# Sparse attention and a PReLU layer pair: a shorter result ring, local q and k turned by transfers, layer-1 order

## The chip, the cores and the metric

The kernel runs on one core of a Trainium2 chip. A core has TensorE (PE, matrix products into the accumulation memory PSUM), VectorE (DVE), ScalarE (ACT), GpSimd (POOL) and SyncE (SP), each with its own instruction queue, and transfers (DMA) that SP and POOL issue. The metric is the device time of one execution in microseconds (us); less is better.

## The reference, cut to what matters

There are 8 batches, 8 heads, 576 positions and 64 values a head. The first four heads use a local mask, the others a strided one. The attention result of all batches, 4608 rows of 512 values, then goes through two linear layers with a PReLU between them.

```python
scores = scale * np.matmul(q, k.transpose(0, 1, 3, 2))
rel = pos[:, None] - pos[None, :]
mask_local = (rel >= 0) & (rel < 32)
mask_strided = (rel >= 0) & (pos[None, :] % 32 == pos[:, None] % 32)
# heads 0 to 3 local, 4 to 7 strided; masked scores to -1e9; softmax; times v
x = attn_out.transpose(0, 2, 1, 3).reshape(B * S, H * D)     # 4608 x 512
h = x @ w_in                                                 # 4608 x 2048
g = np.maximum(h, 0.0) + alpha * np.minimum(h, 0.0)
return g @ w_out                                             # 4608 x 512
```

## The kernel before, in words

**Two streams on one core.** The two layers work on nine chunks of 512 rows (`n` = 0 to 8). Attention works on batches of 576 rows, and within a batch on four pairs of heads: two local ones, then two strided ones (`hp` = 0 to 3). The order of instructions on every engine is written out by hand: the loop over `n` at L902 emits layer-1 and layer-2 pieces of a chunk and, between them, attention pieces of batch `n + 1` from the list `pieces`, which the loop at L532 fills. Pair `g` of the whole list belongs to batch `c = g // 4`. While chunk `n` is in work, the list stands at batch `c = n + 1`.

**Attention pieces.** `score_both` (L381) makes a pair's scores on PE, takes exponentials on ACT (L414, L420, the second ones deferred to later steps) and multiplies by the mask on POOL (L416, L423). `pv_piece` (L428) multiplies by v on PE (L444); DVE then normalizes (L451, L453) into `x16`. PSUM for v products, transposes and half of the scores comes from one pool of three banks (`ps`).

**Getting q and k transposed.** Scores need q and k with the head's values down the partitions. Strided heads of batches 2 to 7 are loaded by POOL (`load_d`, L123) into `qsd` and `ksd`, and two transposing transfers on SP turn them (`transpose_d`, L130). Local heads are loaded as 32-bit rows (`load_qk`, L116), cast by POOL (`cast_l`, L185), transposed on PE (`transpose_piece`, L241, and `tails`, L271) and copied out of PSUM by ACT and DVE. In the lists of pieces these are `T` and `Tk`.

**Results into the ring.** The attention result has to be transposed as well before layer 1 reads it. Of a batch's four pairs the first three go by a transposing transfer (`x_dma`, L472); the third of them also needs a reordering copy on ACT (`x_copy`, L483), and the fourth is transposed on PE (`x_piece`, L461, "xp") and copied by ACT (L465). The target `xT` is a ring of `RING = 3 * S` = 1728 rows. A chunk of 512 rows can lie across the ring's end, as chunks 3 and 6 do; `lin1_piece` then splits each matmul in two.

**Layer 1.** `lin1_piece(n, m)` (L616) makes block `m` of 16 (128 hidden columns each): four matmuls of 512 columns into a bank `hps` of a pool of three, a Relu on ACT (L636) and a combining step on DVE (L639) that writes block `m` of `gT`. That last step is put on a list `late`, and `attn_step` (L604) emits it after the attention piece of the step.

**Layer 2.** From chunk 2 on `lin2_fast` (L716) forms the 2 x 2 block product with seven products instead of eight. Product "5" multiplies `gsum[0]` by `wsum[0]`, "6" takes `gsum[1]`, "7" `gsum[2]` and "3" `gsum[3]`; "1", "2" and "4" read `gT` itself. The products come in the order 1, 5, 6, 2, 7, 3, 4, in two halves of rows each. `g_sum(n, i, h, eng)` (L686) forms half `h` of `gsum[i]` from `gT`, on DVE or POOL: `gsum[0]` from the odd and even blocks of the second row half, `gsum[1]` from `gsum[0]`, `gsum[2]` from even blocks alone, `gsum[3]` from `gsum[1]`. The table `sums` (L898) says after which piece of a chunk which half is emitted and on which engine.

Of the kernel before, what the change touches and what calls it, by code (L numbers as in the profile page):

```python
# [10 lines left out]
F16 = mybir.dt.float16  # L11
# [20 lines left out]
def kernel(  # L32
# [10 lines left out]
    nc = tc.nc  # L43
    keep = tc.keep_in_program_order
# [2 lines left out]
    NT = B * S  # L47
    NCH = NT // 512
    SCALE = 1.0 / float(np.sqrt(D))
    RING = 3 * S  # L50

    consts_dram = nc.inline_tensor(_build_consts(), name="consts").ap()

# [35 lines left out]
    DX = 2  # L89
# [12 lines left out]
    def load_qk(b, strided, nm):  # L102

        h0 = 4 if strided else 0
        src = q if nm == "q" else k
        if strided and b:
            t16 = hpool.tile([128, 2, 512], F16, tag=f"{nm}s", bufs=2, name=f"{nm}s")
            cast16[(b, True, nm)] = t16  # L110
        else:
            t16 = hpool.tile([128, 2, 512], F32, tag=f"{nm}l", bufs=2, name=f"{nm}l")
            loaded[(b, strided, nm)] = t16
        base = src[b, h0 : h0 + 1, 0:1, :]
        eng = nc.sync if (b > 2 and not strided) or (b == 0 and strided) else nc.gpsimd
        keep(eng.dma_start(t16, bass.AP(  # L116
            tensor=base.tensor, offset=base.offset,
            ap=[[8 * D, 64], [2 * S * D, 2], [S * D, 2], [1, 8 * D]])))

    def load_d(b):  # L120

# [306 lines left out]
    def pv_piece(P, a):  # L428
# [12 lines left out]
        for x in range(nb):  # L441
# [13 lines left out]
            pvv[:, :, 0:64],  # L455
            rc[0:w, 0:nb].unsqueeze(2).to_broadcast([w, nb, 64]), op=ALU.mult))

    def x_piece(P):
        xp = pspool.tile([128, 1024], F16, tag="ps", name="xp")
        for t in range(P.n):  # L460
            keep(nc.tensor.transpose(  # L461
                xp[:, P.w * t : P.w * t + P.w], P.x16[0 : P.w, 128 * t : 128 * t + 128], ident[0 : P.w, 0 : P.w]))
        base = (P.b % 3) * S
        if P.strided:
            keep(nc.scalar.copy(  # L465
                xT[:, P.hp, base : base + S].rearrange("r (p t) -> r p t", t=8),
                xp[:, 0:576].rearrange("r (t p) -> r p t", t=8)))
        else:
            cast_copy("act" if P.b < NEARLY and P.hp == 0 else "dve",
                      xT[:, P.hp, base : base + S], xp[:, 0:576])  # L470

    def x_dma(P):  # L472
        base = (P.b % 3) * S
        if P.strided:
            P.xs = xpool.tile([128, 8, 80], F16, tag="xs", bufs=2, name="xs")
            keep(nc.sync.dma_start_transpose(P.xs, P.x16[0:80, :]))
        else:
            keep(nc.sync.dma_start_transpose(
                xT[:, P.hp, base : base + S].rearrange("r (w p) -> r w p", p=96), P.x16[0:96, 0:768]))

    def x_copy(P):
        base = (P.b % 3) * S
        keep(nc.scalar.copy(  # L483
            xT[:, P.hp, base : base + S].rearrange("r (p t) -> r p t", t=8),
            P.xs[:, :, 0:72].rearrange("r t p -> r p t")))

    npair = 4 * B
    pairs = [make_pair(g) for g in range(npair)]
# [43 lines left out]
    for g in range(7, npair + 2):  # L532
        c = g // 4
        a, p, t = g, g - 1, g + 1
        okA = 8 <= a < npair
        okP = 8 <= p < npair
        okT = 8 <= t < npair and (t % 4 == 0 or t < 4 * DX and t % 2 == 0)
        nP = len(pairs[p].pgroups) if okP else 0
        seq = []
        if okA:  # L540
            seq.append(("S", lambda a=a: score_both(pairs[a])))
        if okP:
            seq.append(("P", Pv(p, 0)))
# [12 lines left out]

        todo = [(c, pr) for pr in range(2)] if g % 4 == 0 and 8 <= g < npair else []

        if g % 4 == 1 and 9 <= g and c + 1 < B:
            todo = [(c + 1, nm) for nm in "qk"]  # L560
        lastP = max([i for i, z in enumerate(seq) if z[0] == "P"], default=len(seq) - 1)
        nslots = [i for i, z in enumerate(seq) if z[0][0] != "S"] or list(range(len(seq)))
        for i, (kind, fn) in enumerate(seq):
            extra = []
            if todo and i in nslots:
                left = len([z for z in nslots if z >= i])
                cnt = -(-len(todo) // max(1, left))
                extra = [todo.pop(0) for _ in range(min(cnt, len(todo)))]

            def run(fn=fn, extra=extra, g=g, c=c, kind=kind, lastp=(i == lastP), first=(i == 0)):  # L570
                fn()
                for b, pr in extra:
                    if pr in ("q", "k"):
                        cast_l(b, pr)
                        if b + 1 < B:
                            load_qk(b + 1, False, pr)
                        continue
                    cast_v(b, pr, "pool")
                    if pr == 1 and b + 1 < B:
                        load_v(b + 1, True)  # L580
                if kind == "Tk" and g % 4 == 3 and c + 3 < B:
                    load_tail(c + 3, False)
                if lastp:
                    if 4 * DX <= g - 1 < npair and pairs[g - 1].xd:
                        x_dma(pairs[g - 1])
                    if g % 4 == 3 and DX <= c + 1 < B:
                        transpose_d()
                    if g % 4 == 2 and DX <= c and c + 1 < B:
                        load_d(c + 1)
                    if g % 4 == 1 and DX < c and c + 1 < B:  # L590
                        load_v(c + 1, False)
                if first and 4 * DX <= g - 3 < npair and pairs[g - 3].xd and pairs[g - 3].strided:
                    x_copy(pairs[g - 3])
            feed(run, g - 2 if kind == "X" else -1)

# [6 lines left out]
    late = []  # L602

    def attn_step(end):  # L604
        if pos["i"] < end:
            pieces[pos["i"]][1]()
            pos["i"] += 1
        while late:
            late.pop(0)()
        if defer:  # L610
            defer.pop(0)()

# [1 line left out]
    gTs = {}  # L614

    def lin1_piece(n, m):  # L616
        if m == 0:
            gTs[n] = gpool.tile([128, 16, 512], F16, tag="gT", name="gT")
        c0 = (512 * n) % RING
        parts = [(c0, 0, min(512, RING - c0))]  # L620
        if c0 + 512 > RING:
            parts.append((0, RING - c0, 512 - (RING - c0)))
        hps = phpool.tile([128, 512], F32, tag="hps", name="hps")
        for kk in range(4):
            for x, (src, dst, w) in enumerate(parts):
                keep(nc.tensor.matmul(  # L626
                    hps[:, dst : dst + w],
                    win16[:, kk, 128 * m : 128 * m + 128],
                    xT[:, kk, src : src + w],
                    start=(kk == 0 and x == 0),  # L630
                    stop=(kk == 3 and x == len(parts) - 1),
                    skip_group_check=True,
                ))
# [258 lines left out]
    while pos["i"] < end1:  # L892
# [3 lines left out]

    FAST = 2
    sums = {  # L898
        9: [(0, 0, "pool")], 12: [(2, 0, "pool")], 15: [(0, 1, "dve"), (1, 0, "dve")],
        16: [(1, 1, "dve")], 18: [(2, 1, "dve")], 19: [(3, 0, "dve")], 20: [(3, 1, "dve")]}  # L900

    for n in range(1, NCH):  # L902
        ab = attn_until(n + 1) if n + 1 < B else len(pieces)
# [1 line left out]
        acc = 0.0  # L905
        for i in range(32 if n < FAST else 30):
            if i < 16:
                lin1_piece(n, i)
            elif n < FAST:
                lin2_piece(n, i - 16)  # L910
            else:
                lin2_fast(n, i - 16)
            acc += left / (22 if n < FAST else 19.5 if n == B - 2 else 21) * (0.5 if i < 16 else 1.0)
            cnt = int(acc)
            acc -= cnt
            attn_n(cnt, ab)
# [38 lines left out]
```

## Time and profile before

| what | value |
|---|---|
| runs: median, lowest, highest of 3 | 324.15, 320.11, 325.09 us |
| the profiled execution's own time | 319.59 us |
| its span, first to last instruction | 317.8 us |
| PE busy | 304.1 us, 96% |
| DVE busy | 218.6 us, 69% |
| ACT busy | 182.7 us, 58% |
| POOL busy | 175.6 us, 55% |
| granted TensorE clock, mean | 0.999 |
| read from memory, written | 38.01 MB, 9.44 MB |

The span is what the profile's positions refer to. Chunks start on PE near 28, 66, 83.5 (layer 2 of chunk 1), 102, 134, 166, 198, 231, 261 and 287 us; the last two have no attention beside them. In a row of groups, the text reads: line, engine, operation, what is written and read, shapes, count | busy us, mean ns of one | idle time of the engine just before, and what ended it. In a row of the timeline: start, duration, engine, line, operation, count, and in brackets the idle time before and who ended it. In a row by windows: the window and its length, busy us of PE, weight loads, DVE, ACT and POOL with counts, the granted clock, the DMA share and GB/s. Matmul durations are those of single pipelined instructions and overlap; the time one costs is from its start to the start of the next.

### The profile page before, as it was taken

The page shows a single profiled execution, that of the slowest core. Times are in us where ns is not written, and L with a number is a line of the kernel's source. Part 1 is how long each engine was busy: PE and PEld are TensorE (multiplying, and loading weights), DVE is VectorE, ACT ScalarE, POOL GpSimd, SP SyncE. Part 2 cuts the span into 40 slices and gives each one's busy share as a digit, 9 for nine tenths or more (in the row PEclk, how much of TensorE's full clock was granted, in tenths as well). Part 3 has the DMA queues.
Part 4 walks back from the last instruction along what each step waited for, and adds up shares of the span by engine and source line. Part 5 has one row for each costly group of instructions (what it writes and reads, how often), then busy time and mean ns, then how long its engine had stood idle before and what let it go on. Part 6 is the DMA issues. An engine that isn't in the chain of part 4 may idle for free.

```text
span 317.8 us, 7200 instructions
## 1 busy us (share of the span) xinstructions
PE 304.1 (96%) x2877; PEld 195.9 (62%) x2877; DVE 218.6 (69%) x407; ACT 182.7 (58%) x337; POOL 175.6 (55%) x168
## 2 busy tenths in 40 slices
PE   7699989999999999999999999999999999999994
PEld 2365446554454448887884488448866784685483
DVE  5356864547786888478857885789568958835851
ACT  1464656468555766577557755765566446525630
POOL 8772387437969974967496729673808300400500
PEclk9999999999999999999999999999999999999999
DMA  6999999999597992999199909980920040011003
GB/s 207 197 203 207 216 197 160 179 213 235 93 149 164 248 109 31 179 254 117 21 140 285 133 8 170 162 101 2 171 87 19 3 122 33 0 62 72 2 6 127
DMA packets 81057, 40.38 MB, mean 127 GB/s; under 512 B 58480, under 2 KB 76160, under 8 KB 81024
## 3 DMA queue, kind: packets, MB, share of 16 engines
q0 software_dynamic: 41728, 17.38, 48.2%
q1 hardware_dynamic: 39296, 22.55, 31.4%
q8 instruction: 22, 0.36, 0.5%
q14 instruction: 11, 0.09, 0.1%
HBM read 38.01 MB, written 9.44 MB: 149 GB/s over the span
## 4 chain that ended last, share of the span: by engine, by line
PE 69%; DVE 14%; ACT 7%; issue 4%; DMA 2%; POOL 2%; SPq 0%; ACTq 0%; DVEq 0%
PE hps L626 29%; PE ops L753 21%; PE ops L667 7%; DVE gT L639 5%; PE pv L444 3%; DVE gsum L697 3%; DMA kl<-in_k_dram 2%; ACT xT L483 2%; DVE x L453 2%; ACT et L420 2%; PE sp L401 2%; PE wps L795 2%; PE xp L461 1%; ACT neg L636 1%; PE tp L241 1%
## 5 line engine op out<-in xcount | busy, mean ns | idle before, releaser
L626 PE MATMUL hps<-xT,win 128*128 128x512 f16 (+2 forms) x704 | 133.1, 340 | 0.6
L639 DVE SCALAR_TENSOR_TENSOR gT<-neg,oma,hps 128x512 f16<-128x512 f32 x144 | 105.5, 744 | 39.8 <-ACT neg L636 29.6
L636 ACT ACTIVATE neg<-hps 128x512 f32<-128x512 f32 x144 | 86.1, 598 | 38.8 <-PE hps L626 36.4
L626 PEld LDWEIGHTS <-win 128*128 128x128 f16 x704 | 62.8, 98 | 54.9 <-issue 1.6
L416 POOL TENSOR_TENSOR et<-et,consts 128x576 f16<-128x576 f16 (+1 forms) x24 | 30.7, 1279 | 58.3 <-ACT et L414 55.5
L697 POOL TENSOR_TENSOR gsum<-gT 128x1024 f16<-128x1024 f16 x14 | 29.7, 2128 | 40.5 <-DVE gT L639 40.5
L753 PEld LDWEIGHTS <-gsum 128*128 128x128 f16 x448 | 41.3, 98 | 7.6 <-DVE gsum L697 3.0
L753 PE MATMUL ops<-wsum,gsum 128*128 128x256 f16 x328 | 41.7, 273 | 1.0 <-DVE gsum L697 0.8
L451 DVE RECIPROCAL rc<-pv 72x6 f32<-72x6 f32 (+2 forms) x80 | 14.8, 185 | 30.3 <-PE pv L444 30.0
L753 PEld LDWEIGHTS <-gT 128*128 128x128 f16 x336 | 31.1, 98 | 6.8 <-DVE gT L639 1.6
L453 DVE TENSOR_TENSOR x<-pv,rc 96x384 f16<-96x384 f32 (+2 forms) x62 | 33.0, 532 | 2.1
L667 PE MATMUL ops<-wout,gT 128*128 128x512 f16 x128 | 32.5, 379 | 0.0
L423 POOL TENSOR_TENSOR et<-et,consts 128x576 f16<-128x576 f16 (+1 forms) x24 | 30.9, 1286 | 0.6 <-ACT et L420 0.6
L444 PEld LDWEIGHTS <-et 72*128 72x128 f16 (+1 forms) x448 | 24.0, 98 | 10.6 <-POOL et L423 0.8
L753 PE MATMUL ops<-wout,gT 128*128 128x256 f16 x224 | 29.2, 273 | 0.5
L414 ACT ACTIVATE et<-sp 128x576 f16<-128x576 f32 (+1 forms) x24 | 15.5, 646 | 12.9 <-PE sp L401 12.9
L420 ACT ACTIVATE et<-sph 128x288 f16<-128x288 f32 (+1 forms) x48 | 18.4, 411 | 0.0
L795 PE MATMUL wps<-wrm 128*128 128x512 f16 x44 | 16.3, 448 | 1.2 <-DVE wrm L807 1.2
L770 ACT COPY par<-ops 128x512 f32<-128x512 f32 x13 | 7.6, 586 | 16.9 <-PE ops L753 16.9
L706 ACT COPY osb<-ops 128x512 f32<-128x512 f32 x14 | 8.2, 586 | 15.7 <-PE ops L753 15.7
L185 POOL COPY vs<-stv 72x1024 f16<-72x1024 f16 x14 | 16.4, 1176 | 0.0
L667 PEld LDWEIGHTS <-gT 128*128 128x128 f16 x128 | 10.7, 97 | 8.7
(106 smaller groups left out, 342.6 us busy)
## 6 DMA issues: line engine op xcount, KB each, us to landing
out_dram<-osb SPq DMA_DIRECT2D x35, 256.0 KB, 3.2
ql<-in_q_dram SPq DMA_DIRECT2D x6, 512.0 KB, 6.0
kl<-in_k_dram SPq DMA_DIRECT2D x6, 512.0 KB, 7.4
stv<-in_v_dram POOLq DMA_DIRECT2D x8, 288.0 KB, 7.9
vl<-in_v_dram POOLq DMA_DIRECT2D x6, 384.0 KB, 7.6
win<-in_moe_w_in_dram POOLq DMA_DIRECT2D x4, 512.0 KB, 10.9
wout<-in_moe_w_out_dram POOLq DMA_DIRECT2D x4, 512.0 KB, 14.0
qsd<-in_q_dram POOLq DMA_DIRECT2D x6, 288.0 KB, 6.9
```

The source lines that it names most:

```text
L416: keep(nc.gpsimd.tensor_tensor(mv, mv, m, op=ALU.mult))
L420: keep(nc.scalar.activation(ev[:, n * y : n * y + n], sps[y][0:r, 0:n], AF.Exp, scale=SCALE))
L423: keep(nc.gpsimd.tensor_tensor(mv, mv, m, op=ALU.mult))
L444: keep(nc.tensor.matmul(pv[:, 65 * x : 65 * x + 65], et[0:r, c : c + 128], v16[0:r, 2 * P.pr + hh, t, :] if P.strided else v16[:, 6 * (2 * ...
L453: keep(nc.vector.tensor_tensor(P.x16[0:w, c0 : c0 + 64 * nb].rearrange("r (c e) -> r c e", e=64), pvv[:, :, 0:64], rc[0:w, 0:nb].unsqueeze ...
L626: keep(nc.tensor.matmul(hps[:, dst : dst + w], win16[:, kk, 128 * m : 128 * m + 128], xT[:, kk, src : src + w], start=(kk == 0 and x == 0) ...
L636: keep(nc.scalar.activation(neg, hps, AF.Relu, scale=-1.0))
L639: keep(nc.vector.scalar_tensor_tensor(gTs[n][:, m, :], neg, oma[:, m : m + 1], hps, op0=ALU.mult, op1=ALU.add))
L667: keep(nc.tensor.matmul(ops, gTs[n][:, kf, 128 * mt : 128 * mt + 128], wout16[:, kf, :], start=(kf == 0), stop=(kf == 15)))
L697: keep((nc.vector if eng == "dve" else nc.gpsimd).tensor_tensor(gsum[i][:, hs], a, b, op=op))
L753: keep(nc.tensor.matmul(o, lhs(y), rhs(y), start=(first and y == 0), stop=(y == 7), skip_group_check=True))
L795: keep(nc.tensor.matmul(wps, wrm[:, 0:128], wrm, start=True, stop=True))
```

## The change

1. `RING` becomes 3 * 512 = 1536 rows, so that a chunk never lies across its end and `lin1_piece` loses its split. Batches 2 and 5 now lie across the end, and their transfers and copies into `xT` are made in two parts (`spans`).
2. For local heads of batches 5 to 7 (`NX` = 5), `load_rows` has POOL load the rows of each head as 16-bit, four transfers for q and four for k, in the pieces of pair `g % 4 == 2` two batches ahead. `turn_rows` issues four transposing transfers on SP after the scores of the third pair of the batch before. The casts, the row-tail loads, the PE transposes and the copies of these three batches are gone.
3. Layer 1 of chunks 2 to 8 makes the even blocks first, and `sums` changes: both halves of `gsum[2]` are on POOL and early, then POOL's half of `gsum[0]`; DVE has one half sum less.
4. `attn_step` emits the entries of `late` ahead of the attention piece instead of behind it.
5. `x_copy` moves from the first to the third piece of a pair's pieces.

The lists have 15 attention pieces a batch instead of 17 where `T` and `Tk` are gone, and the spreading over a chunk follows from that.

```diff
-    RING = 3 * S
+    RING = 3 * 512
...
+    NX = 5
+    def load_rows(b, nm):
+        src = q if nm == "q" else k
+        t16 = hpool.tile([128, 2048], F16, tag=f"{nm}l", bufs=2, name=f"{nm}r")
+        for h in range(4):
+            base = src[b, h : h + 1, 0:1, :]
+            keep(nc.gpsimd.dma_start(
+                t16[0:96, 768 * (h // 2) : 768 * (h // 2) + 768].rearrange(
+                    "p (w h d) -> p w h d", w=6, h=2)[:, :, h % 2, :],
+                bass.AP(tensor=base.tensor, offset=base.offset, ap=[[D, 96], [96 * D, 6], [1, D]])))
+        loaded[(b, False, nm)] = t16
+    def turn_rows(b):
+        for nm in "qk":
+            t16 = loaded[(b, False, nm)]
+            for e in range(2):
+                o = qTs[0][:, e, 0:576] if nm == "q" else kTs[0][:, e, 32:608]
+                keep(nc.sync.dma_start_transpose(
+                    o.rearrange("r (w p) -> r w p", p=96), t16[0:96, 768 * e : 768 * e + 768]))
...
+    def spans(b):
+        d0 = b * S % RING
+        w = min(S, RING - d0)
+        return [(0, d0, w)] + ([(w, 0, S - w)] if w < S else [])
...
-        okT = 8 <= t < npair and (t % 4 == 0 or t < 4 * DX and t % 2 == 0)
+        okT = 8 <= t < npair and t < 4 * NX and (t % 4 == 0 or t < 4 * DX and t % 2 == 0)
...
+        elif g % 4 == 2 and c + 2 < B and c + 2 >= NX:
+            todo = [(c + 2, nm) for nm in "qk"]
...
                     if pr in ("q", "k"):
-                        cast_l(b, pr)
-                        if b + 1 < B:
+                        if b > c + 1:
+                            load_rows(b, pr)
+                            continue
+                        if b < NX:
+                            cast_l(b, pr)
+                        if b + 1 < NX:
                             load_qk(b + 1, False, pr)
...
-                if kind == "Tk" and g % 4 == 3 and c + 3 < B:
+                if first and g % 4 == 2 and NX <= c + 1 < B:
+                    turn_rows(c + 1)
+                if kind == "Tk" and g % 4 == 3 and c + 3 < NX:
                     load_tail(c + 3, False)
...
-                if first and 4 * DX <= g - 3 < npair and pairs[g - 3].xd and pairs[g - 3].strided:
+                if second and 4 * DX <= g - 3 < npair and pairs[g - 3].xd and pairs[g - 3].strided:
                     x_copy(pairs[g - 3])
...
     def attn_step(end):
+        while late:
+            late.pop(0)()
         if pos["i"] < end:
             pieces[pos["i"]][1]()
             pos["i"] += 1
-        while late:
-            late.pop(0)()
...
     sums = {
-        9: [(0, 0, "pool")], 12: [(2, 0, "pool")], 15: [(0, 1, "dve"), (1, 0, "dve")],
-        16: [(1, 1, "dve")], 18: [(2, 1, "dve")], 19: [(3, 0, "dve")], 20: [(3, 1, "dve")]}
+        5: [(2, 0, "pool")], 9: [(2, 1, "pool")], 12: [(0, 0, "pool")], 15: [(0, 1, "dve"), (1, 0, "dve")],
+        16: [(1, 1, "dve")], 18: [(3, 0, "dve")], 19: [(3, 1, "dve")]}
...
-                lin1_piece(n, i)
+                lin1_piece(n, i if n < FAST else 2 * (i % 8) + i // 8)
```

More of the change, by code (lines that the diff above doesn't have):

```diff
@@ L462, in x_piece @@
                 xp[:, P.w * t : P.w * t + P.w], P.x16[0 : P.w, 128 * t : 128 * t + 128], ident[0 : P.w, 0 : P.w]))
[L463 to L470, printed above, removed]
+        for s0, d0, w in spans(P.b):
+            o = xT[:, P.hp, d0 : d0 + w]
+            if P.strided:
+                keep(nc.scalar.copy(
+                    o.rearrange("r (p t) -> r p t", t=8),
+                    xp[:, 0:576].rearrange("r (t p) -> r p t", t=8)[:, s0 // 8 : (s0 + w) // 8, :]))
+            else:
+                cast_copy("act" if P.b < NEARLY and P.hp == 0 else "dve", o, xp[:, s0 : s0 + w])
     def x_dma(P):
-        base = (P.b % 3) * S
         if P.strided:
@@ L477, in x_dma @@
         else:
-            keep(nc.sync.dma_start_transpose(
-                xT[:, P.hp, base : base + S].rearrange("r (w p) -> r w p", p=96), P.x16[0:96, 0:768]))
+            for s0, d0, w in spans(P.b):
+                keep(nc.sync.dma_start_transpose(
+                    xT[:, P.hp, d0 : d0 + w].rearrange("r (w p) -> r w p", p=96),
+                    P.x16[0:96, 128 * (s0 // 96) : 128 * ((s0 + w) // 96)]))
     def x_copy(P):
[L482 to L485, printed above, removed]
+        for s0, d0, w in spans(P.b):
+            keep(nc.scalar.copy(
+                xT[:, P.hp, d0 : d0 + w].rearrange("r (p t) -> r p t", t=8),
+                P.xs[:, :, s0 // 8 : (s0 + w) // 8].rearrange("r t p -> r p t")))
     npair = 4 * B
@@ L568, with run @@
                 extra = [todo.pop(0) for _ in range(min(cnt, len(todo)))]
-            def run(fn=fn, extra=extra, g=g, c=c, kind=kind, lastp=(i == lastP), first=(i == 0)):
+            def run(fn=fn, extra=extra, g=g, c=c, kind=kind, lastp=(i == lastP), first=(i == 0),
+                    second=(i == min(2, len(seq) - 1))):
                 fn()
@@ L616, in lin1_piece @@
     def lin1_piece(n, m):
-        if m == 0:
+        if n not in gTs:
             gTs[n] = gpool.tile([128, 16, 512], F16, tag="gT", name="gT")
         c0 = (512 * n) % RING
-        parts = [(c0, 0, min(512, RING - c0))]
-        if c0 + 512 > RING:
-            parts.append((0, RING - c0, 512 - (RING - c0)))
         hps = phpool.tile([128, 512], F32, tag="hps", name="hps")
         for kk in range(4):
[L625 to L633, printed above, removed]
+            keep(nc.tensor.matmul(
+                hps, win16[:, kk, 128 * m : 128 * m + 128], xT[:, kk, c0 : c0 + 512],
+                start=(kk == 0), stop=(kk == 3)))
         neg = npool.tile([128, 512], F32, tag="neg", name="neg")
```

## The prediction

> **What bounds the kernel now.** I read the page first: TensorE (PE) is busy 96% of the span and holds 69% of the chain that ended last.
>
> ```profile
> span 317.8 us, 7200 instructions
> PE 304.1 (96%) x2877; PEld 195.9 (62%) x2877; DVE 218.6 (69%) x407; ACT 182.7 (58%) x337; POOL 175.6 (55%) x168
> PE 69%; DVE 14%; ACT 7%; issue 4%; DMA 2%; POOL 2%; SPq 0%; ACTq 0%; DVEq 0%
> ```
>
> Then I read the timeline of chunk 4 (166.3 to 198.4 us; chunks 2 to 5 look alike, 32.1 us each). PE first: `S` marks the scores of the third pair of a batch, and the row with gsum is product "5", the first that reads gsum[0].
>
> ```profile
> 170.94 0.30 PE L401 MATMUL sp<-qT,kT 64*128 64x72 f16 x8
> 182.14 1.35 PE L753 MATMUL ops<-wout,gT 128*128 128x256 f16 x8
> 183.33 0.61 PE L241 MATMUL tp<-consts,ql 128*128 128x128 f16 x8
> 184.83 2.14 PE L753 MATMUL ops<-wsum,gsum 128*128 128x256 f16 x16
> 197.28 0.42 PE L461 MATMUL xp<-consts,x 72*128 72x72 f16 x8
> ```
>
> PE goes from S (170.94) to product "5" (184.83) in 13.9 us with hardly a gap. Adding up, from 60 us to the end, by how much matmuls start later than their columns take, I get 13 us: that is all that better overlap could ever give. Per chunk the waits over 0.2 us are four: a layer-1 bank 0.28, the last gT at the start of layer 2 0.30, gsum 0.22, and the bank for xp 0.31. Now POOL in the same stretch:
>
> ```profile
> 172.30 1.26 POOL L416 TENSOR_TENSOR et<-et,consts 72x576 f16<-72x576 f16 x1 [2.52 <-ACT et L414]
> 173.54 1.26 POOL L423 TENSOR_TENSOR et<-et,consts 72x576 f16<-72x576 f16 x1
> 174.76 0.80 POOL L123 DMA_DIRECT2D qsd<-in_q_dram  x1
> 175.55 0.73 POOL L123 DMA_DIRECT2D ksd<-in_k_dram  x1
> 176.29 2.14 POOL L697 TENSOR_TENSOR gsum<-gT 128x1024 f16<-128x1024 f16 x1
> 180.30 1.26 POOL L416 TENSOR_TENSOR et<-et,consts 72x576 f16<-72x576 f16 x1 [1.88 <-ACT et L414]
> ```
>
> The row at 176.29 is POOL's half of gsum[0]. It is done at 178.4, 6.4 us before PE wants it. That slack is what the change spends.
>
> **The change, part by part.**
>
> *Ring.* Chunks 3 and 6 no longer split their layer-1 matmuls. A pair of 384 and 128 columns starts 0.219 us apart in sum, an unsplit one 0.216; 128 pairs give 0.4 us. The split moves to the stores of batches 2 and 5, two copies or transfers each, on ACT and SP beside PE.
>
> *Turned by transfers.* For batches 5 to 7, 18 transposes of 128 columns at 0.056 us leave PE: 1.0 us a batch, 3.0 in all. ACT loses the copies (1.01 and 0.28 us), POOL two casts (1.03 each) and two tl issues (0.65 each). SP gains four transposing transfers a batch, issued after S and wanted by the next batch's first scores (18.4 us later, 170.94 to 189.33). In the trace one such lands after 5.2 to 8.3 us, and two issued 1.4 us apart landed 2.0 us apart, so four take some 12 us: hidden. If each had to end before the next starts, 4 x 6.3 = 25 us would come out some 2 us late even after the stall below; I keep 6 us over three chunks as that end.
>
> POOL gains eight row loads for each of batches 5 to 7, issued in chunks 2, 3 and 4. Their rows are not in the trace; the nearest are these.
>
> ```profile
> L173 POOL DMA_DIRECT2D vl<-in_v_dram x8 | 11.2, 1405 | 5.5 <-PE pv L444 4.4 <-DMA tl<-in_q_dram 1.0 <-POOL vs L827 0.2
> L155 POOL DMA_DIRECT2D tl<-in_q_dram x8 | 5.2, 655 | 1.8 <-DMA wout<-in_moe_w_out_dram 1.8
> L123 POOL DMA_DIRECT2D qsd<-in_q_dram x6 | 4.7, 791 | 0.0
> ```
>
> Issues of 256 short runs (tl) take 0.65 us, of 2304 (the first vl) 1.20, of 3072 1.50; the lowest POOL issue is 0.55. A row load has 576 runs: 0.65 + 0.55 x 320/2048 = 0.73. Ends: 0.55 and 1.50. Eight cost 5.8 us, and in the timeline POOL does nothing else while it issues.
>
> *Even blocks first, sums moved.* gsum[2] leaves DVE: 0.68 us less per chunk there, 2.13 more on POOL. What matters is the place. By the changed program's order POOL does, in chunks 3 and 4: first mask of S, gsum[2] first half, second mask, four row loads, gsum[2] second half, four row loads, qsd, ksd, and only then its half of gsum[0]. That is 2 x 1.26 + 2 x 2.13 + 8 x 0.73 + 1.52 + 2.13 = 16.3 us from the first mask, which starts 1.36 us after S (170.94 to 172.30): ready at S + 17.6. PE after S has ten blocks at 0.864 (8.6), four pv groups (0.8), two score groups (0.9) and two products (1.7): it stands at product "5" at S + 12.0. In the trace matmuls start in the order of the program, so PE stands still for 5.6 us, and DVE's gsum[1] waits behind the same half. In chunk 2 another mask and no split of the loads give S + 18.9 against PE's S + 13.3: 5.6 again. Three chunks: **+16.8 us**. Behind gsum[0] wait the masks of the fourth pair, 2.6 us; PE wants them 3.9 us after product "5" starts, so they add nothing. At 0.55 an issue the sum is 12.5, at 1.50 it is 35, too far from the nearest shape to use; I take 0.65 to 0.80 as likely.
>
> Chunk 5 loads no rows: gsum[0] is ready 5.8 us earlier and meets PE.
>
> *Layer-1 results first.* The layer-1 bank (0.28) and last-gT waits (0.30) of chunks 2 to 5 go: -2.3. The gsum waits of chunks 2 to 4 go under the stall, and chunk 6's (0.95) halves: -1.2. In chunk 5 the cover of the eight transposes is gone from ahead of gsum[0]'s DVE half, +0.7 to 1.1: +0.9.
>
> *x_copy.* It moves from the score piece to the piece with xp.
>
> ```profile
> 195.61 1.30 ACT L483 COPY xT<-xs 128x576 f16<-128x576 f16 x1
> 197.73 0.64 ACT L465 COPY xT<-xp 128x576 f16<-128x576 f16 x1 [0.21 <-PE xp L461]
> ```
>
> So xp no longer waits (0.31 five times, less one, and 0.52 once: -1.8). But the 1.30 copy now follows the 0.64 one, ending 0.45 + 0.64 + 1.25 = 2.3 us after xp starts on PE, while PE has only one product and two matmuls (0.26 + 0.88 + 0.43 = 1.6) before the third layer-1 matmul of the next chunk reads that tile: 0.8 us a chunk. Four chunks, and 0.7 for the two with more cover: +4.0 (ends 0 and 5).
>
> Sum: 16.8 - 3.0 - 0.4 - 2.3 - 1.2 + 0.9 - 1.8 + 4.0 = **+13.0 us** on the profiled execution's 319.6 (317.8 of span and 1.8 around it): 332.6. The three runs shown reach from 320.1 to 325.1 with their median 4.6 above the profiled one; I add half of that and forecast 335.
>
> **A stall of 5.6 us and the clock.** In this trace the clock fell in the tail, where PE's last matmul ended near 313.5:
>
> ```profile
> 314.00:316.00 2.00, 0.00 (x0) 0.00 (x0) 0.00 (x0) 0.00 (x0) 0.00 (x0) 1.00 0.59 201
> 316.00:317.00 1.00, 0.00 (x0) 0.00 (x0) 0.00 (x0) 0.00 (x0) 0.00 (x0) 0.92 0.00 0
> 317.00:317.80 0.80, 0.00 (x0) 0.00 (x0) 0.00 (x0) 0.00 (x0) 0.00 (x0) 0.50 0.00 0
> ```
>
> (the granted clock is the column before the last two). A mean of 0.92 puts the fall at 316.8, after 3.3 us without work; the idle 2.1 us near 9 us left the speed alone. At the start matmuls of 512 columns came every 0.43 us, half speed, until 4.9 us of work were done. The Trainium skill (TensorE: Matmul & The Clock Gate, "The HAM clock gate") says that an idle window of about 3.4 us halves the clock and a busy one restores it, the windows running free; the trace agrees, and by it a 5.6 us gap holds a whole window about six times in ten.
>
> **The rivals.**
> 1. *The clock falls in the stalls too.* For: 5.6 is over 3.3. Against: 3.3 is one case. Each fall costs up to 4.9 / 2 = 2.4 us, three 7.3: 342 on the forecast's footing.
> 2. *The stall is hidden.* PE loses nothing if the half sum is there at S + 12.0, for which a load may cost 0.03 us. Then 13.0 - 16.8 = -3.8: 318, within 2%. Against it stands every POOL issue row. The Trainium skill (DMA: Bandwidth & Descriptors, "Anatomy of one DMA") puts dispatch at about 50 ns and descriptor generation at "small, variable"; by its figure eight loads would cost 0.4 us and this would be the result, but the rows have 0.55 to 1.50.
> 3. *The other side: faster.* One mechanism, cheap issue. The total turns to a gain below 0.20 us an issue (1.3 us of stall a chunk, the 3.8 of gains used up). With no stall, and x_copy's 4.0 covered as well because ACT is then ahead, -7.8: 314 on the forecast's footing. For: all four wait rows go away. Against: no row is under 0.55.
> 4. *The turned transfers come late*, one after another: +6, 341. For: one landed only after 8.3 us beside loads. Against: the pair that landed 2.0 apart.
>
> **How the numbers follow.** Forecast 0.42, rival 1 0.25, rival 2 0.17, rival 3 0.08, rival 4 0.08. Slower by over 2% (6.4 us, about what a measurement here can tell from no change) are the forecast and rivals 1 and 4: 0.75; within it rival 2: 0.17; faster rival 3: 0.08. The forecast's own range is 328 to 339 (issue at 0.55 to 0.80, x_copy 0 to 5). The range wanted is 322 to 345: it leaves out rival 3 and most of rival 2, and takes in rivals 1 and 4.
>
> **What would show it.** Right: in chunks 2 to 4 PE idles 5 to 6 us ahead of product "5", released by POOL gsum; eight POOL issues of some 0.73 us between a batch's third and fourth pair; chunk 5 near 32 us; x_copy last ahead of layer 1. Wrong: PE waits for gsum under 1.5 us there, or the row loads issue in under 0.3 us.

## The result, and the profile after

The changed kernel takes 343.56 us, the median of 4 runs from 340.83 to 345.92; four runs of the kernel before have 323.43 (320.11 to 325.09). The ratio is 1.066, with a 95% interval from 1.052 to 1.080: slower. Executions of one kernel differ by over 2% with the granted clock (spans of the kernel before run from 315.1 us at 0.999 to 322.9 us at 0.976), so a ratio is taken from fast runs and need not be the quotient of the medians beside it. The profiled execution took 342.24 us with a span of 340.1, against 319.59 and 317.8 before.

First the page of the changed kernel: its head, the row of the granted clock in 40 slices, the shares of the chain that ended last, and two groups of part 5 (count, then busy us, mean ns of one, and idle time before with its releaser).

```profile
span 340.1 us, 6867 instructions
PE 310.1 (91%) x2695; PEld 190.5 (56%) x2695; DVE 223.3 (66%) x397; ACT 176.4 (52%) x332; POOL 200.9 (59%) x187
...
PEclk9769999999999997999789995999999999999999
...
PE 64%; POOL 15%; DVE 7%; issue 6%; ACT 5%; DMA 2%; SPq 0%; POOLq 0%; ACTq 0%; DVEq 0%
...
L783 PE MATMUL ops<-wsum,gsum 128*128 128x256 f16 x328 | 47.4, 299 | 17.7 <-POOL gsum L727 16.0
...
L727 DVE TENSOR_TENSOR gsum<-gsum,gT 128x1024 f16<-128x1024 f16 x14 | 15.3, 1119 | 10.6 <-POOL gsum L727 10.6
```

POOL holds 15% of the chain instead of 2%, and 16.0 of the 17.7 us that PE idles in front of the products that read `gsum` are ended by POOL's `gsum`, in three waits. PE has 182 instructions fewer, yet is busy 6 us longer, and the clock row dips in slices where it was full before. Now chunk 3 in the timeline (143.9 to 182.9 us), PE first: the scores of the third pair of the batch ("S"), the last work ahead of product "5", and product "5".

```profile
150.11 0.30 PE L424 MATMUL sp<-qT,kT 64*128 64x72 f16 x8
...
161.03 1.04 PE L783 MATMUL ops<-wout,gT 128*128 128x256 f16 x8
161.91 0.35 PE L467 MATMUL pv<-vs,et 72*128 72x65 f16 x6
167.62 3.60 PE L783 MATMUL ops<-wsum,gsum 128*128 128x256 f16 x16 [5.37 <-POOL gsum L727]
```

And POOL in the same stretch:

```profile
151.47 1.27 POOL L439 TENSOR_TENSOR et<-et,consts 72x576 f16<-72x576 f16 x1 [5.81 <-ACT et L437]
152.71 2.12 POOL L727 TENSOR_TENSOR gsum<-gT 128x1024 f16<-128x1024 f16 x1
154.79 1.27 POOL L446 TENSOR_TENSOR et<-et,consts 72x576 f16<-72x576 f16 x1
156.01 2.95 POOL L128 DMA_DIRECT2D qr<-in_q_dram  x4
158.97 2.14 POOL L727 TENSOR_TENSOR gsum<-gT 128x1024 f16<-128x1024 f16 x1
161.05 2.90 POOL L128 DMA_DIRECT2D kr<-in_k_dram  x4
163.94 0.76 POOL L146 DMA_DIRECT2D qsd<-in_q_dram  x1
164.68 0.74 POOL L146 DMA_DIRECT2D ksd<-in_k_dram  x1
165.42 2.15 POOL L727 TENSOR_TENSOR gsum<-gT 128x1024 f16<-128x1024 f16 x1
```

POOL is never idle from the first mask to the half of `gsum[0]` that PE waits for (165.42). Before, that half ended 6.4 us ahead of PE; now it ends at 167.6, and PE has stood still since 162.1. Counted from the time at which the next matmul was due to start, as PE's waits are in the text below, that is 5.53 us here (the row's 5.37 counts from the modelled end of the last one), 5.40 in chunk 2 and 5.53 in chunk 4.

The windows of the changed kernel show what else came with it (length; busy us of PE, PEld, DVE, ACT, POOL with counts; granted clock, DMA share, GB/s). The first is the lead-in, then chunks 3, 4 and 5, then four pieces around the stall of chunk 3.

```profile
0.00:31.60 31.60, 26.74 (x235) 14.10 (x235) 15.60 (x47) 12.41 (x25) 20.05 (x35) 0.84 1.22 207
143.86:182.87 39.01, 33.02 (x299) 21.54 (x297) 23.95 (x43) 18.71 (x36) 28.30 (x26) 0.91 0.97 117
182.87:221.23 38.36, 32.37 (x298) 21.21 (x296) 23.95 (x43) 18.72 (x37) 28.19 (x26) 0.91 0.94 121
221.23:253.86 32.63, 30.88 (x299) 19.94 (x297) 24.62 (x43) 18.62 (x38) 22.22 (x17) 1.00 0.83 131
...
163.20:166.60 3.40, 0.00 (x0) 0.00 (x0) 0.00 (x0) 0.00 (x0) 3.40 (x5) 1.00 1.28 81
166.60:167.60 1.00, 0.00 (x0) 0.00 (x0) 0.00 (x1) 0.00 (x0) 1.00 (x2) 0.50 0.58 83
167.60:173.40 5.80, 5.78 (x38) 4.00 (x40) 5.70 (x10) 0.59 (x1) 2.87 (x2) 0.50 0.52 83
173.40:175.00 1.60, 1.60 (x28) 1.40 (x23) 0.21 (x2) 1.23 (x3) 0.68 (x1) 0.99 0.57 101
```

After a window of 3.4 us without a matmul the clock is halved, and PE then works 5.8 us at half speed.

From start to start of layer 1 the chunks changed so: chunk 1 by -0.45 us, chunks 2, 3 and 4 by +5.8, +6.7 and +6.3, chunk 5 by +0.6, chunk 6 by -0.5, chunk 8 by -0.6. Ahead of them lies a lead-in that is 4.45 us longer in this execution, at half clock from 13.0 to 23.2 us; its code is unchanged, and eight of the ten kernels run below have such a stretch there too, of 3.4 to 13.7 us. All this adds up to the 22.3 us between the two spans.

### The profile page after: what moved, and what is told of

It reads as the page before. It is cut to its first block, busy times and chain, and to the rows that moved or that the text cites. A ratio compares the mean times of both kernels' runs of the same rounds, so it can differ in the third digit from the quotient of the medians.

```text
span 340.1 us, 6867 instructions
## 1 busy us (share of the span) xinstructions
PE 310.1 (91%) x2695; PEld 190.5 (56%) x2695; DVE 223.3 (66%) x397; ACT 176.4 (52%) x332; POOL 200.9 (59%) x187
## 4 chain that ended last, share of the span: by engine, by line
PE 64%; POOL 15%; DVE 7%; issue 6%; ACT 5%; DMA 2%; SPq 0%; POOLq 0%; ACTq 0%; DVEq 0%
PE hps L661 23%; PE ops L783 22%; PE ops L697 7%; POOL gsum L727 4%; PE pv L467 3%; POOL kr L128 2%; DMA kl<-in_k_dram 2%; PE wps L825 2%; POOL qr L128 2%; DVE gT L669 2%; POOL et L446 2%; ACT neg L666 2%; POOL et L439 1%; PE sp L424 1%; POOL vs L208 1%
## 5 line engine op out<-in xcount | busy, mean ns | idle before, releaser
L661 PE MATMUL hps<-xT,win 128*128 128x512 f16 x576 | 131.9, 379 | 2.1 <-ACT xT L513 1.9
L661 PEld LDWEIGHTS <-win 128*128 128x128 f16 x576 | 54.1, 98 | 62.8 <-issue 3.7
L727 POOL TENSOR_TENSOR gsum<-gT 128x1024 f16<-128x1024 f16 x21 | 44.8, 2135 | 42.5 <-DVE gT L669 36.7
L783 PE MATMUL ops<-wsum,gsum 128*128 128x256 f16 x328 | 47.4, 299 | 17.7 <-POOL gsum L727 16.0
L439 POOL TENSOR_TENSOR et<-et,consts 128x576 f16<-128x576 f16 (+1 forms) x24 | 31.8, 1325 | 51.4 <-ACT et L437 51.2
L783 PEld LDWEIGHTS <-gsum 128*128 128x128 f16 x448 | 44.2, 104 | 26.8 <-POOL gsum L727 16.3
L783 PEld LDWEIGHTS <-gT 128*128 128x128 f16 x336 | 31.5, 98 | 5.4 <-issue 0.3
L446 POOL TENSOR_TENSOR et<-et,consts 128x576 f16<-128x576 f16 (+1 forms) x24 | 32.9, 1370 | 0.0
L727 DVE TENSOR_TENSOR gsum<-gsum,gT 128x1024 f16<-128x1024 f16 x14 | 15.3, 1119 | 10.6 <-POOL gsum L727 10.6
L738 DVE TENSOR_TENSOR osb<-ops,par 128x512 f32<-128x512 f32 (+1 forms) x14 | 9.4, 672 | 17.3 <-issue 8.9
L196 POOL DMA_DIRECT2D vl<-in_v_dram x8 | 11.3, 1413 | 11.7 <-PE pv L467 10.2
```

The source lines that it names most:

```text
L439: keep(nc.gpsimd.tensor_tensor(mv, mv, m, op=ALU.mult))
L446: keep(nc.gpsimd.tensor_tensor(mv, mv, m, op=ALU.mult))
L661: keep(nc.tensor.matmul(hps, win16[:, kk, 128 * m : 128 * m + 128], xT[:, kk, c0 : c0 + 512], start=(kk == 0), stop=(kk == 3)))
L727: keep((nc.vector if eng == "dve" else nc.gpsimd).tensor_tensor(gsum[i][:, hs], a, b, op=op))
L783: keep(nc.tensor.matmul(o, lhs(y), rhs(y), start=(first and y == 0), stop=(y == 7), skip_group_check=True))
```

## The experiments

Each comparison has its own runs of the kernel before, on its own chip, so ratios are to be compared and not times. The edits are made to the changed kernel.

**The eight row loads later.** They go behind the last v product of the fourth pair, that is behind `gsum[0]` on POOL.

```diff
-        elif g % 4 == 2 and c + 2 < B and c + 2 >= NX:
-            todo = [(c + 2, nm) for nm in "qk"]
...
+                if lastp and g % 4 == 3 and NX <= c + 2 < B:
+                    for nm in "qk":
+                        load_rows(c + 2, nm)
```

> The changed kernel with one thing moved: the eight row loads of a batch are issued on POOL behind its half of gsum[0] and the masks of the fourth pair, not ahead of them. The number of loads, turned transfers and bytes is the same. Theory 1 (POOL's order makes gsum[0] late): the half of gsum[0] is ready 11.8 us after S in chunks 3 and 4 where PE wants it at 12.0, and 13.1 against 13.3 in chunk 2, so the three waits of 5.4 to 5.5 us ahead of product 5 shrink below 0.5 us, the clock keeps to full speed there, and chunks 2 to 4 take 31 to 32.5 us instead of 37.9 to 39.0; the profiled span falls to 316 to 321 us. Rival A (the row loads and turned transfers themselves slow the chunk, by transfers in flight or by arriving late): as many are in flight, so chunks 2 to 4 stay above 35 us and the span above 330 us.

Measured: 327.2 us, ratio 1.028 (1.016 to 1.041); span 322.3. Every wait of PE for POOL is gone. Chunks 2 to 5 take 31.90, 37.48, 33.04 and 33.22 us. The span misses what was expected mostly because of chunk 3, where a new wait stands (chunk 4 is above the expected 32.5 too, with some 2 us of waits for DVE's sums); here are ACT's row and PE's in the timeline of this kernel.

```profile
136.87 0.59 ACT L737 COPY osb<-ops 128x512 f32<-128x512 f32 x1 [3.38 <-DMA out_dram<-osb]
```

```profile
137.50 1.02 PE L662 MATMUL hps<-xT,win 128*128 128x512 f16 x4 [2.52 <-ACT osb L737]
```

The copy of a chunk's last product needs one of three result buffers, and the store of an earlier one had not landed; the clock fell too. SP issues that chunk's four stores behind three transposing transfers, and the first landed after 6.7 us. The transposing transfers alone don't explain it: in the kernel before the same three stand ahead of a chunk's stores, and the first store landed after 3.1, 3.6 and 3.0 us (chunks 2 to 4). What differs is POOL's load of the next values (`stv`, 288 KB). Here are the load and the stores at the end of chunk 2, in this kernel and then in the kernel before:

```profile
129.34 0.81 POOL L188 DMA_DIRECT2D stv<-in_v_dram  x1
130.02 7.83 SPq L743 DMA_DIRECT2D out_dram<-osb  x4
```

```profile
129.49 1.77 SPq L712 DMA_DIRECT2D out_dram<-osb  x2
130.76 0.81 POOL L165 DMA_DIRECT2D stv<-in_v_dram  x1
```

In the kernel before the two stores ahead of the load landed after 3.1 and 3.3 us, and the two that follow it after 6.8 and 7.5. In all kept traces together, the first store of chunks 2 to 4 landed after 3.0 to 4.6 us where the load was issued 0.45 us or more behind it (15 cases), and after 6.3 to 7.5 where it was issued as much ahead of it (7 cases); with less between them both occur (14 cases). No run moved that load alone.

**The old table of sums and the old block order.** The row loads stay where the change puts them.

```diff
-        5: [(2, 0, "pool")], 9: [(2, 1, "pool")], 12: [(0, 0, "pool")], 15: [(0, 1, "dve"), (1, 0, "dve")],
-        16: [(1, 1, "dve")], 18: [(3, 0, "dve")], 19: [(3, 1, "dve")]}
+        9: [(0, 0, "pool")], 12: [(2, 0, "pool")], 15: [(0, 1, "dve"), (1, 0, "dve")],
+        16: [(1, 1, "dve")], 18: [(2, 1, "dve")], 19: [(3, 0, "dve")], 20: [(3, 1, "dve")]}
...
-                lin1_piece(n, i if n < FAST else 2 * (i % 8) + i // 8)
+                lin1_piece(n, i)
```

> The changed kernel with part 3 undone: layer-1 blocks in natural order and the half sums in the places and on the engines of the kernel before; row loads where the change put them. Theory 1: POOL's half of gsum[0] now has only masks and four loads ahead of it in chunks 3 and 4 (ready 8.9 us after S, wanted at about 12) and masks, eight loads, qsd and ksd in chunk 2 (13.4 against 13.3): no wait at product 5 but for up to 0.5 us in chunk 2. The mask of the fourth pair is then behind the loads and gsum[2], ready at 16.8 us after S where PE wants it at 15.9: waits of about 1 us in chunks 3 and 4 at that v product. Chunks 2 to 4 at 31.5 to 33.5 us, the span 318 to 324 us. Rival B (the eight issues alone cost it, wherever the sums stand): chunks 2 to 4 stay above 35 us.

Measured: 328.13 us, ratio 1.031 (1.025 to 1.036). In the profiled execution, which took 336.59 us against 327.4 to 328.7 for the other three, chunks 2 to 5 take 36.0, 35.7, 35.3 and 34.5 us, so these lengths are not those of the median. PE no longer waits for POOL's half, but for DVE's, 3.4 us in chunk 2. DVE and POOL there, in two views of this kernel's timeline:

```profile
124.19 4.26 DVE L727 TENSOR_TENSOR gsum<-gT 128x1024 f16<-128x1024 f16 x1
```

```profile
122.43 2.16 POOL L727 TENSOR_TENSOR gsum<-gT 128x1024 f16<-128x1024 f16 x1
124.53 1.28 POOL L439 TENSOR_TENSOR et<-et,consts 72x576 f16<-72x576 f16 x1
125.77 2.12 POOL L727 TENSOR_TENSOR gsum<-gT 128x1024 f16<-128x1024 f16 x1
```

A half sum that takes DVE 0.68 us by itself takes 4.26 beside three POOL operations in a row. The loads push POOL's own work into the stretch in which DVE sums, so the old table does not save the kernel. The expected lengths were missed; the rival's 35 us were passed, in that one execution, but not for its reason, since no product waits for POOL.

**PE kept busy in the stall.** Ahead of product "5" of chunks 2 to 4, 16 matmuls of 512 columns whose result nothing reads.

```diff
+                if i == 18 and n in (2, 3, 4):
+                    wsp = pbpool.tile([128, 2, 512], F32, tag="sp", name="wsp")
+                    for _ in range(16):
+                        keep(nc.tensor.matmul(wsp[:, 0], wrm[:, 0:128], wrm, start=True, stop=True))
```

> The changed kernel with work added: 16 matmuls of 512 zero columns into the score bank ahead of product 5 in chunks 2, 3 and 4, 3.5 us of PE work in each of the three waits; nothing reads the result. Theory 1 with the clock (idle of over 3.3 us halves the clock): the added matmuls lie in the wait, idle shrinks to about 2 us, the clock stays at full speed in chunks 2 to 4, and those three chunks together get 6 to 7 us shorter although they do more (half speed lasted 3.2, 5.8 and 4.3 us after PE took up work again, and half of that was lost). Rival C (the halved clock in the records costs nothing, or the wait isn't waiting): the three chunks stay at 37.9, 39.0 and 38.4 us or grow by up to 3.5 us each.

Measured: 343.88 us, ratio 1.081 (1.077 to 1.086). The clock no longer falls in those stalls, but chunks 3 to 5 take 41.3, 39.8 and 37.7 us, because ACT's copies of the last products wait for stores again (2.0 to 3.8 us of PE each), and the clock falls behind two of these waits. Missed, and no verdict on the clock until those waits were out of the way.

**`x_copy` back to its old piece.**

```diff
-                if second and 4 * DX <= g - 3 < npair and pairs[g - 3].xd and pairs[g - 3].strided:
+                if first and 4 * DX <= g - 3 < npair and pairs[g - 3].xd and pairs[g - 3].strided:
```

> The changed kernel with part 5 undone: x_copy is back at the first piece of the pair. Read from the rows, since the total moves by less than the clock does. Prediction's step: the wait of 0.79 us for xT at the third layer-1 matmul of chunks 3, 4 and 6 goes, and xp waits again by 0.3 us for its bank: about 0.5 us less in each of chunks 2 to 5 (measured start to start), 1.5 to 2.5 us in all. Rival D (the wait only moves on, since POOL's half of gsum[0] is what the chunk waits for, and it starts from S): chunks 2 to 4 keep their length within 0.3 us where S isn't earlier.

Measured: 339.76 us in a single run. PE's waits for `xT` (0.79 us in each of chunks 3, 4 and 6) are gone and those for xp are back (0.3 to 0.6 us, five times); a result-buffer wait of 1.1 us appears. Chunks 2 to 6 add up to 177.7 us, as in the changed kernel, and the three POOL waits stay (5.4 to 5.6). So the expected 1.5 to 2.5 us did not come, and the rival's unchanged chunks did not either (38.8, 37.5 and 39.9 us for chunks 2 to 4).

**No turned transfers.** With `NX` = 8 the ring, the block order, the sums and the early results remain.

```diff
-    NX = 5
+    NX = 8
```

> The changed kernel with part 2 undone (no row loads, no turned transfers; casts, tail loads and PE transposes of batches 5 to 7 are back); ring, block order, sums, results first and x_copy as in the change. Theory 1: without the 5.8 us of row loads POOL's half of gsum[0] is ready 11.8 us after S, against 13.3 for PE with its transposes back, so no wait for POOL ahead of product 5; DVE's half sums may still be held for 1 to 2 us by masks that POOL works on at that moment, and the 0.8 us for xT stays. Chunks 2 to 4 at 32 to 34 us, ratio to before 1.00 to 1.02. Rival E (the order of the sums alone would do it): waits of 3 us or more for POOL gsum stay in chunks 2 to 4.

Measured: 322.03 us in 10 runs against 322.78 in 19, ratio 1.002 (0.997 to 1.008). Chunks 2 to 5: 31.91, 32.70, 32.67, 32.23. No wait for POOL is left, as expected. The loss needs the row loads.

**Loads later and a fourth result buffer.** The first experiment and

```diff
-tc.tile_pool(name="op", bufs=3)
+tc.tile_pool(name="op", bufs=4)
```

> The kernel with the loads moved later, with four result buffers (osb) instead of three. There, chunks 3 and 5 lost 2.7 and 0.6 us early in layer 1, where ACT's copy of the last product of the chunk before waited, with the steps behind it. Theory 2: that copy waits for a buffer whose store, issued by SP behind the transposing transfers and landing after 6.7 us instead of 3, is not done; with a fourth buffer the waits go, the clock has no reason to fall near 139 us, chunk 3 takes 33 to 33.5 us instead of 37.5 and the ratio to before falls from 1.028 to about 1.015. Rival F (ACT is late for another reason, or the store's lateness shows up one step on): chunk 3 stays above 35 us.

Measured: 322.1 us in 10 runs, ratio 1.000 (0.995 to 1.005). Chunk 3 with three buffers and with four, by windows:

```profile
132.31:169.79 37.48, 32.63 (x299) 20.29 (x296) 24.76 (x43) 18.64 (x36) 27.23 (x25) 0.95 1.00 126
```

```profile
136.67:169.71 33.04, 30.74 (x299) 19.87 (x296) 24.71 (x43) 18.70 (x36) 27.23 (x25) 1.00 1.17 141
```

The buffer is worth the whole 4.4 us of that chunk, the clock's fall included. The stores land hardly sooner (the first after 6.3 us), but nothing waits for them now. With it the turned transfers bring no gain yet: about 2.2 us a chunk of waits for DVE's `gsum` and 0.8 for `xT` remain.

**Those waits taken out.** Loads later, four buffers, the old sums and block order, and `x_copy` one piece earlier; then the same with `NX` = 8.

```diff
-                    second=(i == min(2, len(seq) - 1))):
+                    second=(i == min(1, len(seq) - 1))):
```

> The candidate that the theories give: the changed kernel with the row loads behind the fourth pair's masks, block order and sums of the kernel before, x_copy at the second piece (between the two late exponentials) and four result buffers. Ring, turned transfers and layer-1 results first stay. Theories 1 and 2: no wait over 0.7 us is left in chunks 2 to 5; they take 30.8 to 31.8 us (32.1 less 1.0 for the transposes, 0.3 for xp, up to 0.3 for the layer-1 bank), the span is 311 to 316 us at an undisturbed start and the ratio to before 0.98 to 0.995. Rival G (turned transfers cost elsewhere what they save on PE): ratio 1.00 or above.

> The same candidate without part 2 (no row loads, no turned transfers). What is left of the change is the ring, the results first and x_copy one piece later, with four result buffers. Theory: chunks 2 to 5 at 31.3 to 31.9 us (32.1 less the waits for xp and the layer-1 bank), span 313 to 317 us at an undisturbed start, ratio 0.985 to 1.00. Set beside the candidate with turned transfers it tells what part 2 is worth where nothing waits for POOL: 0.3 to 1.0 us a chunk in chunks 3 to 5 by theory 1, nothing or a loss by rival G.

Measured: 315.69 us, ratio 0.980 (0.971 to 0.988), and without the turned transfers 318.57, ratio 0.988 (0.981 to 0.995). The first beats both kernels: its interval lies below 1, though a gain of 2% is not certain by it. Its chunks 3, 4 and 5 by windows, and chunk 3 of the second:

```profile
138.57:168.90 30.33, 30.29 (x299) 19.74 (x296) 23.35 (x44) 18.70 (x35) 25.67 (x25) 1.00 1.36 153
168.90:199.21 30.31, 30.27 (x298) 19.73 (x296) 23.34 (x44) 18.73 (x37) 25.58 (x25) 1.00 1.51 161
199.21:229.51 30.30, 30.27 (x298) 19.73 (x296) 23.34 (x44) 18.80 (x36) 20.36 (x16) 1.00 0.98 143
```

```profile
136.69:168.29 31.60, 31.10 (x316) 20.94 (x314) 23.77 (x45) 20.55 (x38) 23.11 (x21) 1.00 0.88 146
```

PE has no idle time left in these chunks of the first, and the turned transfers save 1.3 us in each when nothing waits for POOL (0.3 to 1.0 was expected). The ring, the early results, the place of `x_copy` and the buffer bring 1.2% together without them.

**The fill again, with four buffers.** The changed kernel with the fourth buffer alone, and with the 16 matmuls as well.

> The changed kernel with four result buffers and nothing else: the base for the next run. By theory 1 the three waits for POOL's half of gsum[0] stay at 5.4 to 5.5 us and the clock falls in each; the changed kernel itself shows no wait for a result buffer, so chunks 2 to 4 stay within 0.5 us of 37.9, 39.0 and 38.4 us. If the buffers were what the change is short of, they would shrink by over 2 us.

> The same with the 16 added matmuls of the fill run ahead of product 5 in chunks 2 to 4 (their result is read by nothing). With three buffers the fill kept the clock up there, but chunks 3 to 5 then waited 2.1, 2.0 and 3.8 us for a result buffer. With four those waits go; the waits of 1.15 us for DVE's gsum[1], which half speed had covered, stay. If half speed costs time: chunks 2 to 4 take about 36.7, 37.5 and 37.8 us, together 3 to 4 us less than without the fill, although PE has 10 us more to do. If it costs none (rival C): they are as long as without the fill or longer.

Measured: 338.63 us, ratio 1.065 (1.048 to 1.082), and 337.1, ratio 1.054 (1.033 to 1.075). The times overlap; the windows of chunks 2 to 4 tell them apart, without the fill and with it:

```profile
107.05:144.91 37.86, 32.65 (x315) 21.85 (x314) 29.25 (x44) 19.85 (x40) 32.12 (x29) 0.95 0.85 97
144.91:183.90 38.99, 33.01 (x299) 21.54 (x296) 23.94 (x43) 18.71 (x36) 28.26 (x26) 0.91 1.01 124
183.90:222.24 38.34, 32.36 (x298) 21.23 (x296) 23.95 (x43) 18.70 (x37) 28.16 (x26) 0.91 0.95 118
```

```profile
105.66:142.33 36.67, 34.85 (x331) 22.28 (x330) 29.09 (x44) 19.94 (x40) 32.13 (x29) 1.00 0.87 93
142.33:179.88 37.55, 34.03 (x315) 21.39 (x312) 23.89 (x43) 18.71 (x36) 28.86 (x26) 1.00 1.02 126
179.88:217.43 37.55, 34.02 (x314) 21.37 (x312) 23.88 (x43) 18.70 (x37) 28.75 (x26) 1.00 1.09 123
```

The fourth buffer alone changes nothing, so result buffers are not what the changed kernel loses by. With 16 matmuls more in each chunk the three chunks take 111.8 us instead of 115.2, so the lost clock costs 3.4 us net of the waits that it covers. As expected.

Put side by side, the length of chunk 4 in us tells the whole loss:

| kernel | chunk 4 |
|---|---|
| before | 32.07 |
| turned transfers, nothing waiting | 30.31 |
| and the new sums and `x_copy` (loads later, 4 buffers) | 33.05 |
| and the loads ahead of `gsum[0]`, clock held by the fill | 37.55 |
| and the clock not held (4 buffers) | 38.34 |

## Why the prediction was right, and where it was off

**POOL's order: right, term by term.** Row loads issue in 0.73 us (2.95 and 2.90 for four), the value taken. `gsum[0]` was ready at S + 17.5 (predicted 17.6) and PE stood at product "5" at S + 12.0 (12.0). The three stalls are 5.40 + 5.53 + 5.53 = 16.5 us; the sum had 16.8. Moving the loads behind that half, or leaving them out, removes the stalls, and with the buffer's wait out of the way the kernel is back at the time of before (ratios 1.000 and 1.002).

**The clock: the step that failed.** The sum of +13.0 has no term for it, although the prediction's own working gave a stall of 5.6 us six chances in ten of a fall; three times 0.6 of its 2.4 us would have put some 4 us into the sum. It stood apart as rival 1 with 0.25, close to 0.6 x 0.6 x 0.6, the chance that all three fall. The measured 343.56 us lie above the forecast's own range of 328 to 339, at that rival's 342; only the wider range, which took the rival in, holds them. The clock fell in all three stalls. PE then worked 3.2, 5.8 and 4.3 us at half speed, a loss of half of that, 6.7 us (the rival had up to 7.3; the 2.9 of chunk 3 are more than its 2.4 a fall). The fill recovers 3.4 of it; most of the rest comes back as a wait of 1.15 us for `gsum[1]` in each of chunks 3 and 4, which DVE makes late in any case. The rule for the chance was too mild as well: the working let the clock fall only where a whole window of about 3.4 us is free of work. So it was in chunks 2 and 3, but in chunk 4 the window before the fall still held matmuls, as these rows of the changed kernel's windows show.

```profile
200.70:204.10 3.40, 0.59 (x10) 0.43 (x8) 0.61 (x1) 0.57 (x1) 3.40 (x6) 1.00 1.11 69
204.10:211.00 6.90, 4.34 (x24) 3.18 (x25) 4.30 (x7) 0.59 (x1) 5.41 (x4) 0.51 0.75 95
```

**The sum.** Chunks 2 to 4 grew by 18.8 us: 16.5 of stalls, 6.7 of half clock and 1.6 of `xT` waits make 24.8, which leaves 6.0 for the gains; that is a remainder and not a measurement. The prediction's gains for these chunks, 2.0 for the transposes, 1.7 for layer 1, 0.7 for `gsum` and 0.9 for xp, make 5.3. The lead-in's 4.45 us are in the profiled execution and in no step. The 22.3 us less the lead-in and the whole loss by the clock are 11.2, less the lead-in and what the fill won back 14.4; the 13.0 of the sum lies between. Part of that is luck: the next two terms were mis-sized by 1.8 and 1.3 us in opposite directions. Between the medians the change is 20.1 us.

**`x_copy`: overestimated.** The wait is 0.79 us as worked out, but three times, not four and 0.7: by the code of `spans` only the first part of batch 5's copy, 192 of its 576 rows, is needed at the start of chunk 5, and no wait shows there. Against the xp waits that it removed (2.0 in all in its own experiment) its 2.4 cost 0.4 net, not 2.2.

**Chunk 5: underestimated.** PE waits 2.2 us for DVE's sums (1.10, 0.23 and 0.85), where 0.9 was taken. The prediction priced a half sum at 0.68, but beside POOL's masks it takes longer; these are DVE and POOL in that chunk of the changed kernel:

```profile
238.53 1.98 DVE L727 TENSOR_TENSOR gsum<-gT 128x1024 f16<-128x1024 f16 x1
240.43 1.75 DVE L727 TENSOR_TENSOR gsum<-gsum,gT 128x1024 f16<-128x1024 f16 x1
242.80 0.68 DVE L727 TENSOR_TENSOR gsum<-gsum,gT 128x1024 f16<-128x1024 f16 x1
```

```profile
238.67 1.28 POOL L439 TENSOR_TENSOR et<-et,consts 72x576 f16<-72x576 f16 x1
239.90 1.73 POOL L446 TENSOR_TENSOR et<-et,consts 72x576 f16<-72x576 f16 x1
```

Each of the first two ends 0.55 us after one of the masks, the third, alone, takes 0.68. The trace of before had a row of the kind (183.84, 1.59 us for the first half), and the prediction did not use it. The Trainium skill (SBUF — State Buffer, "Who interferes with whom") says that a VectorE instruction with two inputs in SBUF contends with a GpSimd instruction that reads SBUF; the trace agrees, with 1.98, 1.75 and, in the second experiment, 4.26 us in place of 0.68. No run measured it by itself.

**Transposes off PE: the term was right.** The saving is 1.3 us a chunk instead of 1.0. The transposes themselves take 0.44 + 0.44 + 0.11 us from start to start, the 1.0 of the prediction; the rest is a `gsum` wait at product "5", 0.67 us in the kernel without the turned transfers against short gaps of some 0.3 in the one with them.

**The rivals.** A hidden stall (318) and cheap issue (314) fell with the 0.73 us. Late transfers (341) did not come in the form given: no scores wait for a turned tile. A wait that no rival had came instead, for a result buffer whose store lands late; the changed kernel's own trace has none. By the rows under the first experiment it goes with POOL's `stv` load being issued ahead of the store, and not with the transposing transfers; no run has tested that. The gains of the shorter ring and of the early results were not isolated from each other; chunks 1, 6 and 8, with 0.45 to 0.6 less each, fit them in size.

## What to carry to other kernels

Before a helper engine is given transfers to issue, list what stands behind them in its queue and when the busiest engine wants each of these: here eight issues of 0.73 us made no wait for POOL behind the deadline and one of 5.5 us ahead of it. A gain that removes work from the busiest engine can be kept, here a gain of 2% in place of a loss of 6.6%, by changing only the order and adding a buffer. And a stall of some 5 us is to be priced, in the sum itself, with the half-speed stretch that follows it.

## What the hardware showed unexpectedly

The clock fell after windows that were not empty: with 0.59 us of matmuls in 3.4 us (above), and in the kernel with the loads later with 1.10 us, as its windows show.

```profile
135.20:138.60 3.40, 1.10 (x10) 0.62 (x10) 0.62 (x1) 1.57 (x3) 0.00 (x0) 1.00 1.76 240
138.60:142.00 3.40, 3.33 (x12) 1.15 (x9) 2.88 (x6) 1.19 (x2) 0.00 (x0) 0.50 0.68 102
```

PE had gone back to work at 137.50, 1.1 us before the fall. Waits of 1.9 to 2.1 us (the fill with four buffers) left the clock whole. The Trainium skill (TensorE: Matmul & The Clock Gate, "The HAM clock gate") has free-running windows of 3413 ns, and half speed after an idle one; the trace agrees on the length, since the half-speed stretches here last 3.4 and 6.8 to 6.9 us, but a window that is one third busy can halve the clock as well.

Even more work was not always enough. In three kernels (loads later, and the two with the waits taken out) the clock fell once near 50 us behind a window of which PE's matmuls, mostly the short ones of scores, fill 2.44 of 3.41 us; this is the window in the kernel with the turned transfers, and the next has a clock of 0.50.

```profile
49.05:52.46 3.41, 2.44 (x40) 1.32 (x39) 0.75 (x2) 2.30 (x7) 2.68 (x2) 1.00 0.75 173
```

In the lead-in the window ahead of the changed kernel's fall at 13.0 us held 1.70 us of matmuls, and the same stretch of the kernel before held 1.93 and kept its clock. So the busy time of a window does not by itself tell whether the clock falls, and what does stays open.

DVE's half sum of 0.68 us reached 4.26 us beside three POOL operations in the second experiment, and 6.35 us beside three in chunk 2 of the changed kernel (from 123.42 us, 0.56 us beyond the third of them). A 256 KB store behind the same three transposing transfers landed after 3.1 us or after 6.7, with POOL's `stv` load issued behind it or ahead of it.
